# Sparse attention into a Mish MLP on one core: how the first batch's v is read, and where the second batch's steps stand

## Chip, cores and metric

One core of one Trainium2 chip runs the whole kernel. The metric is the device time of one execution in microseconds (us), lower is better; the time given is the median of several executions. All times inside an execution are counted from the start of the profiled span.

## What is computed

Eight batches of eight heads, 576 tokens, head width 64. Heads 0 to 3 are "local": a token sees itself and the 31 tokens before it. Heads 4 to 7 are "strided": a token sees those at or before it with the same position modulo 32. The attention output, 4608 tokens of 512 features, goes through an MLP with 2048 hidden features. Cut to what matters:

```
mask_local   = (rel >= 0) & (rel < 32)
mask_strided = (rel >= 0) & (pos[None, :] % 32 == pos[:, None] % 32)
attn = exp(scores - max) / (sum + 1e-9)          # scores masked, scale 1/8
x = (attn @ v) as [4608, 512]
h = x @ w_in;  out = (h * tanh(softplus(h))) @ w_out
```

## The kernel before

**Tiling.** The tokens go through the MLP in nine blocks of 512 (loop over `t`, L724). A block is MLP1 (`mlp1`, L543: eight groups `g` of 256 hidden features, each 8 matmuls of 512 columns into one of three PSUM accumulators, then one Mish on ScalarE, L562) and MLP2 (`mlp2`, L571: sixteen groups of four matmuls into two of the accumulators). The four 128-feature slices `cc` of MLP1 are two local ones (0, 1) and two strided ones (2, 3); the order is 2, 3, 0, 1. While the MLP of block `t` runs, the attention of batch `t+1` is put between its matmul groups: a hand-written list of sixteen steps (`attn_steps`, L476) gives, for each MLP2 group, what follows it on the engines. Each engine works through its instructions strictly in the order in which they were written.

**Attention of a batch.** `t_step` (L230) and `t_step_loc0` (L248) transpose q and k on TensorE into a PSUM tile `tr` and have it copied to `kTs`, `qTs`, `kTl`, `qTl`. `qk` (L302) makes the scores and has ScalarE take the exponential into `Ps` (strided) or `Pl` (local). `mask` (L342) multiplies by a 0/1 mask on VectorE; for batch 0 `bias` (L292) adds the mask as a matmul beforehand instead. `pv` and `pv2` (L367, L379) multiply by v. The v tiles have 65 columns a head: 64 of v and one of ones, so that the 65th column of the product `po` is the softmax denominator; VectorE takes its reciprocal (`rden`) and multiplies (`x_s`, `x_l`). `xt` (L393) transposes the result into `xT`, the MLP's input. The PSUM tiles `tr`, `po` of `pv`, `trx` and `fill` share two buffers in turn: a third one waits until the first has been read.

**Local windows.** For the local heads the queries are cut into six windows of 96, and the v tile `vl` holds 128 rows a window: rows 32 to 127 are the window's own (one DMA a head brings them for all windows), rows 0 to 31 are the last 32 of the window before, copied over from rows 96 to 127 (`rows_v_loc01`, L141).

**Batch 0 (L618 to L702)** comes before any MLP work can start. Its loads are issued by GpSimd (POOL) in a fixed order: strided k, q, v, local k, q, local v, then the weights and batch 1. Strided v lands as bf16 in `vsd`, a view of `vs32`; `copy_v_str01` (L145) copies it on VectorE into the 65-column tile `vs`. POOL has eight landing semaphores in turn, so an issue waits until the eighth issue before it has landed. `fill` matmuls (L525) do no work of the result; they stand where TensorE would wait.

**Batch 1** has its q and k transposes on TensorE too (`t_steps1`, L266): the strided four stand in MLP1 of block 0 (L758 to L760), two after group 6 and two after group 7, the last; the local four follow the third and the fourth MLP2 group. From batch 2 on, DMAs transpose (`str_by_dma`, `loc_by_dma`).

Of the kernel before, what the change touches and what calls it, by code (L numbers as in the profile page):

```python
# [12 lines left out]
AF = mybir.ActivationFunctionType  # L13
# [3 lines left out]
NW = 6  # L17
WQ = 96
# [22 lines left out]
def kernel(ctx, tc, q, k, v, moe_w_in, moe_w_out, out):  # L41
# [63 lines left out]
                dst[b % 2][0:PN], src[b, 4:8].rearrange("h (p j) d -> p h (j d)", j=CS)  # L105
            )

    def load_str01(dst, src, b, h0=0):
        for p in (slice(0, 64), slice(64, PN)):
            nc.gpsimd.dma_start(  # L110
                dst[p, h0:4], src[b, 4 + h0:8].rearrange("h (p j) d -> p h (j d)", j=CS)[p]
            )

    def load_qk_loc(b):
# [23 lines left out]
                vl[b % 2][32:128, :, h, 0:D], v[b, h].rearrange("(w p) d -> p w d", p=WQ)  # L138
            )

    def rows_v_loc01(b, hp, eng):  # L141
        x = vl[b % 2][:, :, 2 * hp:2 * hp + 2, 0:D]
        cast(eng, x[0:32, 1:NW], x[96:128, 0:NW - 1])

    def copy_v_str01(b, eng, j0, j1):  # L145
        cast(
# [140 lines left out]
    class Attn:  # L287
# [63 lines left out]

        def pv_mm(self, kind, i, po):
            for h in range(4):
                if kind == "l":
# [7 lines left out]
                nc.tensor.matmul(  # L362
                    po[:, h, :], lhsT=pt[0:n, c0:c0 + 128], rhs=rhs,
                    start=True, stop=True,
                )
# [110 lines left out]
    def attn_steps(b, x, y, z=None):  # L476

        a = Attn(b)
        Q = lambda i_acc, *parts: (lambda: a.qk(parts, i_acc))
        M = lambda kd, i: (lambda: a.mask(kd, i, nc.vector))  # L480
        V = lambda kd, i: (lambda: a.pv(kd, i))
        X = lambda kd, hf: (lambda: a.xt(kd, hf))
        s0, s1, sl2, l0, l1 = ("s", 0), ("s", 1), (("s", 2), ("l", 2)), ("l", 0), ("l", 1)
        if x == y:
            return [
                [], [Q(x, s0)],
                [M(*s0), Q(x, s1)],
                [V("s", 0)],
                [V("s", 1), M(*s1), Q(x, *sl2)],
                [V("s", 2)],  # L490
                [V("s", 3), M("s", 2), M("l", 2), Q(x, l0)],
                [V("s", 4)],
                [V("s", 5), M(*l0), Q(x, l1)],
                [V("s", 6), V("l", 5)],
                [V("s", 7), V("l", 0), M(*l1)],
                [X("s", 0), V("l", 1)],
                [X("s", 1), V("l", 2)],
                [V("l", 3), V("l", 4)],
                [X("l", 0), X("l", 1)], [],
            ]  # L500
# [21 lines left out]
        return r  # L522


    def fill(t, n):  # L525
# [17 lines left out]
    def mlp1(t, accs):  # L543
        gT = g_pool.tile([128, 16, 512], BF16, tag="gT", name="gT")

        held = {}

        def group(g, ccs=(2, 3, 0, 1), us=(0, 1)):
            if g not in held:
                held[g] = acc(accs[g % 3], "psh")  # L550
            ps = held[g]
            for u in us:
                fc = 2 * g + u
                for a, n, o in segs(t):
                    for cc in ccs:
                        nc.tensor.matmul(  # L556
                            ps[:, u, o:o + n], lhsT=w_in[:, cc, fc * 128:(fc + 1) * 128],
                            rhs=xT[:, cc, a:a + n], start=(cc == 2 and o == 0),
                            stop=(cc == 1 and o + n == 512),
                        )  # L560
            if ccs[-1] == 1 and us[-1] == 1:
                nc.scalar.activation(gT[:, 2 * g:2 * g + 2, :], ps[:], AF.Mish)  # L562
        if t == 0:
            return gT, [lambda g=g, c=c: group(g, c) for c in ((2, 3), (0, 1)) for g in range(2)] + [
                lambda g=g: group(g) for g in range(2, 8)
            ]
# [49 lines left out]
    with tc.manual_schedule():  # L616
# [26 lines left out]
        Dv.memset(kTs[0][:, 0:16 * SU].rearrange("p (u n) -> p u n", n=SU)[:, :, PN:], 0.0)  # L643
        Dv.memset(kTs[0][:, 16 * SU:], 0.0)
# [59 lines left out]
        for x in (ks, qs):  # L704
            Dv.memset(x[0][64:SU], 0.0)
        load_qk_str(2)
        for hp in range(2):
            rows_v_loc01(1, hp, Po)
        for dst, src in ((kl, k), (ql, q)):
            to = by_tile(dst[0])  # L710
            for h in range(4):
# [4 lines left out]
        load_v_loc_h(2)  # L716

        def next_loads():
            load_qk_str(3)
            copy_v_str01(2, Po, 0, CS)  # L720
            for hp in range(2):
                rows_v_loc01(2, hp, Po)

        for t in range(NBLK):  # L724
            x, y, z = accs
            if t > 0:
                gT, g1 = mlp1(t, accs)
            ts, at, a1 = [], [], []
            if t == 0:
                ts, at = t_steps1(), attn_steps(1, y, y)  # L730
                at[0] += [lambda: Sc.preload_act_table(AF.Exp)]
                at[0] += [lambda x=x: Dv.memset(x[1][64:SU], 0.0) for x in (ks, qs)]
                at[1] += [lambda: copy_v_str01(1, nc.vector, 0, CS), next_loads]
                at[2] += ts[4:6]
                at[3] += ts[6:8]
                at[9] += [lambda: str_by_dma(2), lambda: loc_by_dma(2)]
                out_accs, accs = (z, x), (y, z, x)
            else:
                if t <= 2:
                    at = attn_steps(t + 1, x, y, z if t == 2 else None)  # L740
                elif t + 1 < B:
                    a1 = str_steps(t + 1)
                    at = loc_steps(t + 1, x, y)
                if t == 1:
                    at[9].append(lambda: str_by_dma(3))
                if t == 2:
                    Dv.memset(x_s[64:96], 0.0)
                if t + 2 < B:
                    at[9].append(lambda: loc_by_dma(t + 2))
                if 1 < t < B - 3:  # L750
                    at[9].append(lambda: str_by_dma(t + 3))
                out_accs, accs = (z, y), (z, x, y)
            for i, g in enumerate(g1):
                g()
                if i < len(a1):
                    for s in a1[i]:
                        s()
                if t == 0:  # L758
                    for n in {6: (0, 1), 7: (2, 3)}.get(i, ()):
                        ts[n]()  # L760
            if t > 0 and t + 2 < B:
                cast_qk_loc(t + 2, Po, Po)
                if 1 < t < B - 3:
# [50 lines left out]
```

## Time and profile before

| | |
|---|---|
| median of 7 runs | 306.63 us (305.76 to 309.08) |
| the profiled execution's own time | 306.01 us |
| its span, first to last instruction | 304.2 us (1.8 us lie around it) |
| TensorE busy | 296.7 us, 98% of the span |
| VectorE / ScalarE / GpSimd busy | 160.5 / 180.6 / 99.9 us |
| one MLP matmul of 512 columns, start to start | 0.2158 us (64 of them in 13.81 us) |

PE is TensorE, DVE is VectorE, ACT is ScalarE, POOL is GpSimd. In a timeline row stand: start, length, engine, line, operation, what it writes and reads, shapes, how many were merged, and in brackets the idle time of the engine before it with what ended it. A matmul's length includes its way through the array; where many follow each other, the distance of their starts is what they cost.

### The profile page before, as it was taken

The page shows a single profiled execution, that of the slowest core. Times are in us where ns is not written, and L with a number is a line of the kernel's source. Part 1 is how long each engine was busy: PE and PEld are TensorE (multiplying, and loading weights), DVE is VectorE, ACT ScalarE, POOL GpSimd, SP SyncE. Part 2 cuts the span into 40 slices and gives each one's busy share as a digit, 9 for nine tenths or more (in the row PEclk, how much of TensorE's full clock was granted, in tenths as well). Part 3 has the DMA queues.
Part 4 walks back from the last instruction along what each step waited for, and adds up shares of the span by engine and source line. Part 5 has one row for each costly group of instructions (what it writes and reads, how often), then busy time and mean ns, then how long its engine had stood idle before and what let it go on. Part 6 is the DMA issues. An engine that isn't in the chain of part 4 may idle for free.

```text
span 304.2 us, 5877 instructions
## 1 busy us (share of the span) xinstructions
PE 296.7 (98%) x2430; PEld 154.5 (51%) x2430; DVE 160.5 (53%) x380; ACT 180.6 (59%) x192; POOL 99.9 (33%) x117
## 2 busy tenths in 40 slices
PE   8979999999999999999999999999999999999995
PEld 3544555544454455445488554445444444444444
DVE  4681478102840087588878887798878850000000
ACT  2676643766466755756965796578668756116501
POOL 8742429530245035403960394028600000000000
PEclk9999999999999999999999999999999999999999
DMA  8999999999898999999969998797520120011011
GB/s 140 161 206 188 203 182 134 142 116 222 170 210 134 224 158 200 216 188 186 163 151 199 188 158 148 148 194 130 133 84 0 64 76 0 2 69 69 0 71 69
DMA packets 97006, 41.81 MB, mean 137 GB/s; under 512 B 79572, under 2 KB 90916, under 8 KB 96980
## 3 DMA queue, kind: packets, MB, share of 16 engines
q1 hardware_dynamic: 71708, 28.84, 53.1%
q0 software_dynamic: 24960, 12.31, 34.7%
q8 instruction: 19, 0.31, 0.5%
q10 hardware_dynamic: 312, 0.28, 0.3%
q14 instruction: 7, 0.06, 0.1%
HBM read 36.82 MB, written 9.44 MB: 152 GB/s over the span
## 4 chain that ended last, share of the span: by engine, by line
PE 89%; DVE 3%; DMA 2%; POOL 2%; issue 1%; ACT 1%; DVEq 0%; ACTq 0%; POOLq 0%
PE psh L556 41%; PE pso L579 35%; PE pso L606 5%; PE po L362 4%; PE ps L324 3%; DMA vl<-in_v_dram 2%; DVE x_l L374 1%; DVE x_s L374 1%; PE trx L401 1%; POOL vl L137 1%; DVE rden L373 1%; POOL ks L110 0%; DVE Pl L346 0%; ACT Ps L338 0%; POOL qs L110 0%
## 5 line engine op out<-in xcount | busy, mean ns | idle before, releaser
L556 PE MATMUL psh<-xT,w_in 128*128 128x512 bf16 (+1 forms) x640 | 130.6, 358 | 1.0 <-ACT xT L179 0.7
L579 PE MATMUL pso<-w_out,gT 128*128 128x512 bf16 x512 | 121.7, 379 | 0.0
L562 ACT ACTIVATE gT<-psh 128x1024 bf16<-128x1024 f32 x72 | 72.5, 1024 | 47.2 <-PE psh L556 47.2
L556 PEld LDWEIGHTS <-w_in 128*128 128x128 bf16 x640 | 60.2, 98 | 56.5 <-issue 1.4
L579 PEld LDWEIGHTS <-gT 128*128 128x128 bf16 x512 | 45.5, 98 | 45.9
L436 DVE STREAM_TRANSPOSE xs_t<-x_s 32x512 bf16<-32x512 bf16 x48 | 33.7, 702 | 0.9
L586 ACT COPY osb<-pso 128x1024 f32<-128x1024 f32 x16 | 17.6, 1097 | 24.7 <-PE pso L579 14.1
L373 DVE RECIPROCAL rden<-po 72x4 f32<-72x4 f32 (+1 forms) x98 | 17.2, 176 | 26.4 <-PE po L362 26.1
L181 POOL CAST kl<-kl 96x768 bf16<-96x768 f32 x10 | 8.8, 905 | 64.5 <-DMA kl<-in_k_dram 56.1
L181 DVE COPY osb<-pso 128x512 f32<-128x512 f32 (+1 forms) x2 | 1.1, 558 | 51.3 <-PE pso L606 51.3
L346 DVE TENSOR_TENSOR Ps<-Ps,consts_sb 72x864 bf16<-72x864 bf16 (+3 forms) x12 | 8.0, 675 | 37.7 <-ACT Ps L338 37.7
L427 DVE STREAM_TRANSPOSE xT<-x_l 32x384 bf16<-32x384 bf16 x48 | 27.3, 569 | 0.7
L374 DVE TENSOR_TENSOR x_s<-po,rden 72x256 bf16<-72x256 f32 x56 | 23.5, 420 | 1.9
L338 ACT ACTIVATE Ps<-ps 72x864 bf16<-72x864 f32 (+3 forms) x21 | 17.4, 861 | 10.4 <-PE ps L324 10.3
L443 ACT COPY xT<-xs_t 128x576 bf16<-128x576 bf16 x8 | 21.4, 2938 | 0.0
L362 PEld LDWEIGHTS <-Ps 72*128 72x128 bf16 x256 | 14.8, 98 | 11.6 <-DVE Ps L346 0.8
L338 ACT ACTIVATE Pl<-ps 128x960 bf16<-128x960 f32 (+1 forms) x20 | 17.1, 876 | 4.0 <-PE ps L324 3.9
L374 DVE TENSOR_TENSOR x_l<-po,rden 96x256 bf16<-96x256 f32 x42 | 17.6, 420 | 1.4
L179 ACT COPY xT<-trx 128x576 bf16<-128x576 bf16 x15 | 9.5, 641 | 14.1 <-PE trx L411 11.4
L362 PE MATMUL po<-vs,Ps 72*128 72x65 bf16 x256 | 17.3, 194 | 0.1
L181 POOL CAST vl<-vl 128x768 bf16<-128x768 f32 (+2 forms) x20 | 15.4, 771 | 4.1 <-DMA vl<-in_v_dram 3.1
L346 POOL TENSOR_TENSOR Ps<-Ps,consts_sb 72x1008 bf16<-72x1008 bf16 (+1 forms) x9 | 14.5, 1645 | 0.1
(91 smaller groups left out, 233.4 us busy)
## 6 DMA issues: line engine op xcount, KB each, us to landing
out_dram<-osb SPq DMA_DIRECT2D x16, 512.0 KB, 4.4
kl<-in_k_dram SPq DMA_DIRECT2D x5, 576.0 KB, 6.9
ql<-in_q_dram SPq DMA_DIRECT2D x5, 576.0 KB, 11.5
vs<-in_v_dram SPq DMA_DIRECT2D x5, 576.0 KB
vl<-in_v_dram SPq DMA_DIRECT2D x5, 576.0 KB, 9.6
w_in<-in_moe_w_in_dram POOLq DMA_DIRECT2D x4, 512.0 KB, 11.1
w_out<-in_moe_w_out_dram POOLq DMA_DIRECT2D x4, 512.0 KB, 15.6
ks<-in_k_dram POOLq DMA_DIRECT2D x7, 288.0 KB, 9.4
```

Of the source, the lines that this page charges most:

```text
L181: eng.tensor_copy(out_, in_)
L338: nc.scalar.activation(pt[0:n, :, 0:nw], t[0:n, :, o0:o0 + nw], AF.Exp, scale=scale)
L346: meng.tensor_tensor(out=pm, in0=pm, in1=mk[0:n, :].unsqueeze(1).unsqueeze(1).to_broadcast([n, 2, nu, w]), op=ALU.mult,)
L362: nc.tensor.matmul(po[:, h, :], lhsT=pt[0:n, c0:c0 + 128], rhs=rhs, start=True, stop=True,)
L373: nc.vector.reciprocal(rden[0:m, :], po[0:m, :, D])
L374: nc.vector.tensor_tensor(out=dst.rearrange("p (h d) -> p h d", h=4), in0=po[0:m, :, 0:D], in1=rden[0:m, :].unsqueeze(2).to_broadcast([m, ...
L427: nc.vector.transpose(dst[32 * q:32 * q + 32, :, :, m:m + 32], src[m:m + 32, :, :, q, :])
L436: nc.vector.transpose(xs_t[32 * q:32 * q + 32, :, :, m:m + 32], src[m:m + 32, :, :, q, :])
L443: nc.scalar.copy(xT[:, 2 + c, t0:t0 + S].rearrange("p (n j) -> p j n", j=CS), xs_t[:, :, c, 0:PN])
L556: nc.tensor.matmul(ps[:, u, o:o + n], lhsT=w_in[:, cc, fc * 128:(fc + 1) * 128], rhs=xT[:, cc, a:a + n], start=(cc == 2 and o == 0), stop= ...
L562: nc.scalar.activation(gT[:, 2 * g:2 * g + 2, :], ps[:], AF.Mish)
L579: nc.tensor.matmul(p[:, ot % 2, :], lhsT=gT[:, fc, 128 * ot:128 * ot + 128], rhs=w_out[:, fc, :], start=(fc == 0), stop=(fc == 15),)
```

## The change

Five things are altered, all of them for batches 0 and 1:

1. **Strided v of batch 0** is read by the matmul as it landed (`vsd`, 64 columns); a second matmul of one column, against a column of ones in `vl`, makes the denominator. The two VectorE copies into `vs` go.
2. **Local v of batch 0** is loaded a window at a time (six DMAs of 96 x 4 x 64 in place of four of 96 x 6 x 64); the row copy is made in two parts, windows 0 to 2 before `xt("s")`, windows 3 to 5 after the first local `pv2`. For batches 1 and 2 one copy on POOL replaces two.
3. **MLP1 of block 0**: for groups 0 and 1 the local slices are done in two token pieces, of 288 and of 224 columns.
4. **Loads**: the second half of batch 0's strided k is one DMA of 72 rows in place of 64 and 8; the first quarter of `w_in` is two DMAs; the first part of `w_out` moves ahead of batch 1's k and q, the second ahead of its local k and q.
5. **Batch 1's list** is its own (`attn_steps1`): the four strided transposes follow the first MLP2 group, the four local ones stand after groups 6 to 8, local scores come singly at groups 9 to 11. The two memsets of `ks[1]`, `qs[1]` go from VectorE to POOL. Batch 0's first `kTl` copy goes from VectorE to ScalarE, and its local bias and score matmuls alternate.

```diff
+    def load_v_loc01(b, w0, w1):
+        for w in range(w0, w1):
+            nc.gpsimd.dma_start(
+                vl[b][32:128, w, :, 0:D], v[b, 0:4, WQ * w:WQ * w + WQ].rearrange("h p d -> p h d")
+            )
-    def rows_v_loc01(b, hp, eng):
-        x = vl[b % 2][:, :, 2 * hp:2 * hp + 2, 0:D]
-        cast(eng, x[0:32, 1:NW], x[96:128, 0:NW - 1])
+    def rows_v_loc01(b, w0, w1, eng):
+        w0, x = max(w0, 1), vl[b % 2]
+        cast(eng, x[0:32, w0:w1, :, 0:D], x[96:128, w0 - 1:w1 - 1, :, 0:D])
...
+                    if self.b == 0:
+                        v0 = D * (CS * h + i)
+                        rhs, tail = vsd[0][:, v0:v0 + D], vl[0][0:PN, 1, 0, D:D + 1]
...
+                if tail is not None:
+                    nc.tensor.matmul(
+                        po[:, h, D:D + 1], lhsT=pt[0:n, c0:c0 + 128], rhs=tail,
+                        start=True, stop=True,
+                    )
...
+        return [
+            [lambda: nc.scalar.preload_act_table(AF.Exp)] + ts[0:4],
+            [Q(y, ("s", 0)), lambda: copy_v_str01(1, nc.vector, 0, CS)],
+            [M("s", 0), Q(y, ("s", 1))],
+            [V("s", 0)],
+            [V("s", 1), M("s", 1), Q(y, ("s", 2))],
+            [V("s", 2), ts[4]],
+            [V("s", 3), M("s", 2), ts[6], ts[5]],
+            [V("s", 4), ts[7]],
+            [V("s", 5), Q(y, ("l", 0))],
+            [V("s", 6), M("l", 0), Q(y, ("l", 1))],
+            [V("s", 7), V("l", 0), M("l", 1), Q(y, ("l", 2))],
+            [X("s", 0), V("l", 1), M("l", 2)],
+            [X("s", 1), V("l", 2)],
+            [V("l", 3), V("l", 5)],
+            [V("l", 4), X("l", 0)],
+            [X("l", 1)],
+        ]
...
+            parts = (0, 288, 0), (288, 224, 288)
+            return gT, [lambda g=g: group(g, (2, 3)) for g in range(2)] + [
+                lambda g=g, p=p: group(g, (0, 1), part=p) for p in parts for g in range(2)
+            ] + [lambda g=g: group(g) for g in range(2, 8)]
...
-        load_str01(ks[0], k, 0, 2)
+        nc.gpsimd.dma_start(ks[0][0:PN, 2:4], k[0, 6:8].rearrange("h (p j) d -> p h (j d)", j=CS))
...
-        load_v_loc_h(0)
-        for f in range(0, 2048, 512):
-            load_w_in(f, f + 512)
+        load_v_loc01(0, 0, NW)
+        for f0, f1 in ((0, 256), (256, 512), (512, 1024), (1024, 1536), (1536, 2048)):
+            load_w_in(f0, f1)
+        load_w_out(0, 1)
         load_qk_str(1)
-        load_w_out(0, 1)
         load_v_str01(1)
+        load_w_out(1, 2)
         load_qk_loc01(1, rows(kl[1]), rows(ql[1]))
-        load_w_out(1, 3)
+        load_w_out(2, 3)
...
-        copy_v_str01(0, Dv, 0, 4)
-        copy_v_str01(0, Dv, 4, 8)
...
-        t_step_loc0(kl0, kTl[:, 0, 32:32 + S], 0, Dv)
+        t_step_loc0(kl0, kTl[:, 0, 32:32 + S], 0, Sc)
...
-        a.bias("l", 0, 1)
-        a.bias("l", 1, 2)
-        a.qk([("l", 0)], 1)
-        a.qk([("l", 1)], 2)
-        a.bias("l", 2, 0)
-        a.qk([("l", 2)], 0)
-        for hp in range(2):
-            rows_v_loc01(0, hp, Dv)
+        for i in range(3):
+            a.bias("l", i, (1, 2, 0)[i])
+            a.qk([("l", i)], (1, 2, 0)[i])
+        rows_v_loc01(0, 0, 3, Dv)
...
         a.pv2("l", 0, 1)
+        rows_v_loc01(0, 3, NW, Dv)
         a.pv2("l", 2, 0)
...
         def next_loads():
+            for x in (ks, qs):
+                Po.memset(x[1][64:SU], 0.0)
...
-                at[0] += [lambda x=x: Dv.memset(x[1][64:SU], 0.0) for x in (ks, qs)]
-                at[9] += [lambda: str_by_dma(2), lambda: loc_by_dma(2)]
+                at[10] += [lambda: str_by_dma(2), lambda: loc_by_dma(2)]
```

More of the change, by code (lines that the diff above doesn't have):

```diff
@@ L106, in load_qk_str, with load_str01 @@
             )
-    def load_str01(dst, src, b, h0=0):
+    def load_str01(dst, src, b):
         for p in (slice(0, 64), slice(64, PN)):
             nc.gpsimd.dma_start(
-                dst[p, h0:4], src[b, 4 + h0:8].rearrange("h (p j) d -> p h (j d)", j=CS)[p]
+                dst[p], src[b, 4:8].rearrange("h (p j) d -> p h (j d)", j=CS)[p]
             )
@@ L353, in pv_mm @@
             for h in range(4):
+                tail = None
                 if kind == "l":
@@ L361, in pv_mm @@
                     pt, c0 = P_s[part][:, i % 2], PN * u
+                    if self.b == 0:
+                        v0 = D * (CS * h + i)
+                        rhs, tail = vsd[0][:, v0:v0 + D], vl[0][0:PN, 1, 0, D:D + 1]
                 nc.tensor.matmul(
-                    po[:, h, :], lhsT=pt[0:n, c0:c0 + 128], rhs=rhs,
+                    po[:, h, 0:rhs.shape[-1]], lhsT=pt[0:n, c0:c0 + 128], rhs=rhs,
                     start=True, stop=True,
                 )
+                if tail is not None:
[3 more added lines that the diff above has]
+                    )
         def pv(self, kind, i):
@@ L483, in attn_steps @@
         s0, s1, sl2, l0, l1 = ("s", 0), ("s", 1), (("s", 2), ("l", 2)), ("l", 0), ("l", 1)
[L484 to L500, printed above, removed]
         r = [
@@ L522, in attn_steps, with attn_steps1 @@
         return r
+    def attn_steps1(y, ts):
+        a = Attn(1)
+        Q = lambda i_acc, *parts: (lambda: a.qk(parts, i_acc))
+        M = lambda kd, i: (lambda: a.mask(kd, i, nc.vector))
+        V = lambda kd, i: (lambda: a.pv(kd, i))
+        X = lambda kd, hf: (lambda: a.xt(kd, hf))
+        return [
[16 more added lines that the diff above has]
+        ]
     def fill(t, n):
@@ L546, in mlp1, with group @@
         held = {}
-        def group(g, ccs=(2, 3, 0, 1), us=(0, 1)):
+        def group(g, ccs=(2, 3, 0, 1), us=(0, 1), part=None):
             if g not in held:
@@ L553, in group @@
                 fc = 2 * g + u
-                for a, n, o in segs(t):
+                for a, n, o in segs(t) if part is None else [part]:
                     for cc in ccs:
@@ L560, in group @@
                         )
-            if ccs[-1] == 1 and us[-1] == 1:
+            if ccs[-1] == 1 and us[-1] == 1 and (part is None or part[2]):
                 nc.scalar.activation(gT[:, 2 * g:2 * g + 2, :], ps[:], AF.Mish)
         if t == 0:
-            return gT, [lambda g=g, c=c: group(g, c) for c in ((2, 3), (0, 1)) for g in range(2)] + [
-                lambda g=g: group(g) for g in range(2, 8)
-            ]
+            parts = (0, 288, 0), (288, 224, 288)
+            return gT, [lambda g=g: group(g, (2, 3)) for g in range(2)] + [
+                lambda g=g, p=p: group(g, (0, 1), part=p) for p in parts for g in range(2)
+            ] + [lambda g=g: group(g) for g in range(2, 8)]
         return gT, [lambda g=g, c=c: group(g, c) for c in ((2, 3), (0, 1)) for g in range(3)] + [
@@ L706 @@
         load_qk_str(2)
-        for hp in range(2):
-            rows_v_loc01(1, hp, Po)
+        rows_v_loc01(1, 0, NW, Po)
         for dst, src in ((kl, k), (ql, q)):
@@ L718, in next_loads @@
         def next_loads():
+            for x in (ks, qs):
+                Po.memset(x[1][64:SU], 0.0)
             load_qk_str(3)
             copy_v_str01(2, Po, 0, CS)
-            for hp in range(2):
-                rows_v_loc01(2, hp, Po)
+            rows_v_loc01(2, 0, NW, Po)
         for t in range(NBLK):
@@ L727 @@
                 gT, g1 = mlp1(t, accs)
-            ts, at, a1 = [], [], []
+            at, a1 = [], []
             if t == 0:
-                ts, at = t_steps1(), attn_steps(1, y, y)
-                at[0] += [lambda: Sc.preload_act_table(AF.Exp)]
-                at[0] += [lambda x=x: Dv.memset(x[1][64:SU], 0.0) for x in (ks, qs)]
-                at[1] += [lambda: copy_v_str01(1, nc.vector, 0, CS), next_loads]
-                at[2] += ts[4:6]
-                at[3] += ts[6:8]
-                at[9] += [lambda: str_by_dma(2), lambda: loc_by_dma(2)]
+                at = attn_steps1(y, t_steps1())
+                at[1].append(next_loads)
+                at[10] += [lambda: str_by_dma(2), lambda: loc_by_dma(2)]
                 out_accs, accs = (z, x), (y, z, x)
@@ L757 @@
                         s()
-                if t == 0:
-                    for n in {6: (0, 1), 7: (2, 3)}.get(i, ()):
-                        ts[n]()
             if t > 0 and t + 2 < B:
```

## The prediction

> **What bounds the kernel now.** I read the slices of the page first, then the page's chain, then the stretches, the waits of TensorE, and last the timeline.
>
> ```profile
> PE   8979999999999999999999999999999999999995
> PEclk9999999999999999999999999999999999999999
> PE 89%; DVE 3%; DMA 2%; POOL 2%; issue 1%; ACT 1%; DVEq 0%; ACTq 0%; POOLq 0%
> ```
>
> TensorE is busy in every slice, at full clock, and is 89% of the chain that ended last. Only TensorE's idle time, or work added to it, can move the end.
>
> ```profile
> 0.00:10.60 10.60, 9.21 (x87) 4.36 (x87) 4.60 (x22) 3.46 (x5) 9.55 (x18) 1.00 0.92 147
> 10.60:21.50 10.90, 9.00 (x171) 6.10 (x172) 9.64 (x19) 8.39 (x12) 6.20 (x9) 1.00 1.48 186
> 21.50:34.70 13.20, 13.15 (x89) 6.54 (x89) 2.66 (x5) 7.40 (x8) 3.75 (x6) 1.00 1.31 193
> 34.70:56.10 21.40, 20.81 (x257) 11.68 (x254) 16.06 (x41) 11.24 (x15) 13.74 (x19) 1.00 1.59 167
> ```
>
> Columns: stretch, length, then busy time of PE, PEld, DVE, ACT, POOL. The change lies in rows two to four (batch 0's attention, MLP1 of block 0, MLP2 of block 0 with batch 1). PE idles 1.9 us in the second, 0.6 in the fourth. Matmul ends are modelled, so I also went by starts: between 34.7 and 56.1 starts come late for a reason other than the matmul before them by 1.36 us, five times (0.24, 0.12, 0.51, 0.31, 0.18), and 0.1 us is lost at each switch to or from the narrow score and q/k transposes.
>
> ```profile
> PE psh L556 <- ACT xT L179: 0.7, 1, 0.7
> PE po L362 <- ACT Pl L338: 0.7, 1, 0.7
> PE tr L253 <- DVE x_s L374: 0.3, 1, 0.3
> ```
>
> The first is the stall before MLP1's local slices that the token pieces aim at; the last is a PSUM buffer not yet read. The copies of strided v, which the change removes, hold nobody: they end at 9.91, and the first `po` at 10.64 waits for ScalarE's exponential.
>
> **Stage A, up to the first whole MLP1 group** (before: 21.55 plus eight matmuls of 0.2158, 23.28).
>
> ```profile
> 10.64 0.42 PE L362 MATMUL po<-vs,Ps 72*128 72x65 bf16 x8
> 13.11 1.18 ACT L179 COPY qTl<-tr 128x576 bf16<-128x576 bf16 x2 [0.60 <-PE tr L253]
> 14.41 0.56 PE L297 MATMUL ps<-consts_sb 128*128 128x480 bf16 x2 [0.27 <-DVE x_s L388]
> 15.22 1.38 DVE L181 COPY vl<-vl 32x640 bf16<-32x640 bf16 x2
> 20.86 0.64 ACT L179 COPY xT<-trx 128x576 bf16<-128x576 bf16 x1 [0.48 <-PE trx L401]
> ```
>
> *Ones column.* 32 more matmuls, each with its own weight load in the instruction order. No row has one column. Above: the `po` row, (0.42 - 0.19)/7 = 0.033 us each, 1.06 in all. Below: nothing, if they pass in the shadow of weight loads. I take 0.033, because a `po` matmul of 65 columns is the nearest row. So each `pv2` is 0.26 longer. The waits for the q/k loads (0.23 and 0.15) swallow part; the fourth strided `pv2` starts at 13.8 instead of 13.25.
> *`kTl` copy to ScalarE.* It fills ScalarE's 0.60 idle before `qTl`: both `kTl` copies 11.87 to 13.07, `qTl` until 14.8 (before 14.29). First local scores at 14.87 (before 14.90), so the exponentials start at 15.3 as before.
> *Bias alternating.* The second pair of 480 columns (0.42 with its switch) stood in that wait; now it follows the first scores. The transposes of `x_s` go from 15.90 to 16.40, VectorE's `xT` from 16.53 to 16.88, the first `x_l` ends at 18.43 instead of 18.09 (+0.34).
> *Row copy in two parts.* The row gives 0.595 and 0.650 for 640 elements, so about 0.5 for windows 0 to 2 (512 elements), hidden while VectorE waits for `xT`; and 0.72 for windows 3 to 5 (768). The latter now stands between the first and second `rden`, and TensorE's second local `pv2` (window 3) waits for it: 18.35 to 19.07, then 0.39 until the next `rden`. Second `x_l` 20.38 (before 18.98), third 21.22 (before 19.81).
> *TensorE behind it.* First two strided MLP1 groups at 19.53 and 20.70 (before 18.42, 19.54), the transposes of `x_l` after each, the last at 21.56 (before 20.40). Token pieces: the first piece's `xT` is ready at 21.55, so the 0.71 stall is gone and MLP1 goes on at 21.82; 8 x (288 columns, 0.1225) + 8 x (224, 0.096) = 1.75 against 1.73. Whole groups from 23.57: **+0.30**. With the ones columns free the same steps give 22.98, -0.30.
> *Loads.* One DMA of 72 rows for k: the 64 and 8 row pieces landed at 5.11 and 5.82, and are wanted at 6.27 behind the `fill`s; nothing lost. [...] Local v landed last at 15.86 before; its wait (0.14 on VectorE) goes, nothing else hangs on it.
>
> **Stage B, MLP1 to the end of MLP2 of block 0** (before 23.28 to 56.13). MLP1's 48 whole matmuls cost 10.36 in both; the four strided transposes (4 x 0.26) change place.
>
> ```profile
> 31.91 0.42 PE L237 MATMUL tr<-consts_sb,ks 72*128 72x72 bf16 x8
> 32.37 0.46 DVE L181 COPY kTs<-tr 128x576 bf16<-128x576 bf16 x1 [8.72 <-PE tr L237]
> 40.85 0.45 PE L253 MATMUL tr<-consts_sb,ql 96*64 96x96 bf16 x12 [0.35 <-DVE x_s L374]
> 45.33 0.72 POOL L181 COPY vl<-vl 32x640 bf16<-32x640 bf16 x1 [0.89 <-DMA vl<-in_v_dram]
> 45.45 0.91 DVE L346 TENSOR_TENSOR Ps<-Ps,consts_sb 72x576 bf16<-72x576 bf16 x1
> ```
>
> *Four transposes in a row.* They have two PSUM buffers. Start s: the first's copy begins s + 0.46 and ends s + 0.92 (rows one and two), and TensorE follows a read buffer by 0.06 (14.35 to 14.41 in stage A): the third starts at s + 0.98, but TensorE was ready at s + 0.52, 0.46 lost. The second copy ends 0.37 after the first, so the fourth waits 0.11 more. Before, MLP1 groups stood between the pairs. **+0.57**, a new wait, with all of MLP2 behind it.
> *The list.* Going through it with the rows' lengths (pso group 0.863; `po` 0.13; `rden` 0.18, `x_s` 0.42; `kTl` 0.74; masks 0.59, 0.64; TensorE to VectorE 0.23), from the fourth transpose on: 0.09 before the second strided scores, 0.14 before the third `pv` (mask), 0.53 before the first `ql` transposes (buffer not read), 0.06 before the second local scores, 0.30 before the first `trx` of `x_l` (buffer). Sum with 0.57: 1.7, against 1.36 before: +0.35. Nine excursions to narrow matmuls instead of six and a half: 5 more switches of 0.1, +0.5. The 1.98 us of memsets leave VectorE, but the second MLP2 group and the exponential end later than VectorE there, so they bring nothing; on POOL they stand before loads whose transposes start at 88.05, over 9 us after landing (78.69). **+0.8**; between +0.3 (only the transposes, switches hidden) and +1.2.
> *Order of loads.* `w_out`'s first part (landed 33.63, wanted at 34.7) goes ahead of batch 1's k and q (29.23, 31.51; wanted at 31.9). The same bytes then land by about 33.6, wanted from 34.8 on; the two `w_in` quarters have smaller packets, bounded by the 768-byte loads of 1.5 to 2.1 us for 288 KB. No wait.
> *Later batches.* The DMA transposes of batch 2 follow one group later, with TensorE equally late: nothing.
>
> Sum: 0.30 + 0.8 = **+1.1 us** on 306.01, 307.1. The profiled run lay 0.6 under the median of 306.63; against that I predict **307.7**.
>
> **Rivals.** *POOL's single row copy meets a mask (slower).* The last row above: while POOL copied (45.33 to 46.05) the 576-element mask took 0.91, though 864 elements take 0.59; it looks held until POOL ended. The change has one copy of 1280 elements (1.44). By my times the mask runs at 44.7, the copy from 45.3, after local v's last landing (45.21). If TensorE is 0.6 later or v earlier, the mask ends at 47.1, the second `kTl` copy behind it at 47.9, and the `pv` that needs its buffer waits from 46.06: +1.9, in all +3.0, 309.6. For: the gap is small. Against: the same bytes precede local v. [...]
> *Loads late (slower).* If batch 1's q lands at 35.5 instead of 33.6, the transposes start 0.5 late: +1.6, 308.2.
> *Ones columns free, switches hidden.* Stage A -0.3, stage B +0.3: 306.6, no change.
> *The stalls really go (faster).* If stage A's idle 1.9 falls to 0.5 and stage B stays: -1.4, 305.2. Against: the row copy and the two-buffer wait, which the order on VectorE and TensorE shows.
>
> **Chances.** Forecast 0.52 (306.9 to 308.4); free columns 0.18; faster rival 0.10, two thirds of it beyond -0.5%; POOL 0.12; loads 0.08. Half a percent is 1.5 us, about what a measurement can tell from no change: faster 0.07, same 0.63, slower 0.30 (POOL, half of the loads, and the top of the forecast). Range 305.5 to 309.4: it leaves out most of the faster rival and the top of POOL's.
>
> **What would show it.** Whole MLP1 groups start near 23.6; no wait of `psh` for `xT`; VectorE's second row copy between two local `rden` and TensorE's `po` waiting for it; about half a microsecond of TensorE waiting for `kTs` copies near 35.5; MLP1 of block 1 from about 57.2 instead of 56.13. Wrong if ones columns start under 0.02 apart, or if the second row copy ends before 18.6.

## The result, and the profile after

The changed kernel takes **307.98 us** in the median (25 runs, 306.73 to 311.68); the kernel before, on the same chips, 306.64 (62 runs, 305.68 to 310.91). The ratio is **1.0050, with a 95% interval of 1.0035 to 1.0065**: about 1.5 us longer. The forecast was 307.7.

The profiled execution of the changed kernel took 309.12 us and so lay above its median; a second profile of the same code, called e1 below, took 307.69. Both are shown, and the working goes by e1. Of some kernels a part of the runs had a lower granted TensorE clock (0.987 to 0.994 in the mean, the others 0.998 or more; in the profiles of f1 to f4 0.50 for 3.41 us or twice that); that is the subject of the run g1, and medians are of all runs unless the text says otherwise.

First the page of the changed kernel, the slices and the chain:

```profile
PE   8889999999999998999999999999999999999995
PE 90%; DVE 4%; DMA 2%; issue 1%; POOL 1%; ACT 1%; ACTq 0%; POOLq 0%
```

TensorE still sets the end. Then the last three of the four stretches shown of before, cut at the same events (first `po`, in MLP1, first `pso`, block 1's MLP1; length, busy time of PE, PEld, DVE, ACT, POOL, granted clock, DMA share, GB/s). The changed kernel's first profile:

```profile
10.90:21.50 10.60, 8.36 (x187) 5.96 (x188) 6.54 (x16) 7.80 (x11) 8.58 (x12) 1.00 1.38 155
21.50:35.00 13.50, 13.50 (x81) 7.15 (x80) 3.98 (x6) 8.34 (x9) 3.57 (x5) 1.00 1.24 194
35.00:58.57 23.57, 22.59 (x285) 13.23 (x284) 14.53 (x41) 11.42 (x15) 16.05 (x20) 1.00 1.54 179
```

and e1:

```profile
10.95:21.50 10.55, 9.25 (x198) 6.51 (x198) 7.44 (x18) 8.21 (x12) 8.16 (x12) 1.00 1.50 172
21.50:33.86 12.36, 12.36 (x71) 6.51 (x70) 3.14 (x3) 7.70 (x8) 3.15 (x5) 1.00 1.31 193
33.86:57.44 23.58, 22.59 (x286) 13.24 (x285) 14.53 (x41) 11.43 (x15) 13.98 (x19) 1.00 1.60 170
```

The last stretch is the same in both, 23.57 and 23.58; it now holds all four strided transposes. The two profiles differ in the two rows above it. The waits of TensorE from 10 to 58 us say why; the first lines of each list, e1 first, then the first profile:

```profile
PE po L372 <- DVE vl L187: 1.1, 1, 1.1
PE tr L259 <- DVE x_s L389: 0.4, 1, 0.4
PE tr L243 <- DVE kTs L187: 0.3, 1, 0.3
```

```profile
PE po L372 <- DVE vl L187: 1.2, 1, 1.2
PE tr L259 <- DMA lq<-in_k_dram: 0.7, 1, 0.7
```

The wait of `psh` for `xT` is gone. Two new ones stand there: `po` for VectorE's row copy (`vl`, L187), and `tr` for the copies `kTs`. The wait for the load `lq` is in the first profile and not in e1 (local k landed at 12.20 there, at 10.94 in e1), and e4 below, with the loads of before, has one of 0.5: it belongs to that execution.

By the starts of the matmuls, stage A (to the first whole MLP1 group) and stage B (from there to block 1's MLP1):

| | first `po` | whole groups | block 1's MLP1 | stage B |
|---|---|---|---|---|
| before | 10.64 | 23.27 | 56.13 | 32.86 |
| after, first profile | 10.94 | 24.64 | 58.57 | 33.93 |
| after, e1 | 10.99 | 23.50 | 57.44 | 33.94 |
| forecast | 10.64 | 23.57 | 57.2 | 33.6 |

### The profile page after: what moved, and what is told of

Its sections match the earlier page's. It is cut to its first block, busy times and chain, and to the rows that moved or that the text cites. A ratio compares the mean times of both kernels' runs of the same rounds, so it can differ in the third digit from the quotient of the medians.

```text
span 307.4 us, 5958 instructions
## 1 busy us (share of the span) xinstructions
PE 298.1 (97%) x2470; PEld 156.3 (51%) x2470; DVE 155.5 (51%) x375; ACT 181.6 (59%) x193; POOL 103.0 (34%) x119
## 4 chain that ended last, share of the span: by engine, by line
PE 90%; DVE 4%; DMA 2%; issue 1%; POOL 1%; ACT 1%; ACTq 0%; POOLq 0%
PE psh L581 40%; PE pso L605 34%; PE po L372 5%; PE pso L632 5%; PE ps L330 3%; DMA lq<-in_k_dram 2%; DVE x_l L389 1%; PE tr L259 1%; PE trx L416 1%; DVE x_s L389 1%; DVE Pl L352 1%; DVE rden L388 1%; PE trx L426 0%; ACT Ps L344 0%; POOL qs L110 0%
## 5 line engine op out<-in xcount | busy, mean ns | idle before, releaser
L581 PE MATMUL psh<-xT,w_in 128*128 128x512 bf16 (+3 forms) x648 | 130.5, 355 | 0.3 <-ACT Ps L344 0.3
L187 POOL CAST kl<-kl 96x768 bf16<-96x768 f32 x10 | 7.9, 820 | 66.0 <-DMA kl<-in_k_dram 66.0
L187 DVE COPY osb<-pso 128x512 f32<-128x512 f32 (+1 forms) x2 | 1.1, 558 | 51.3 <-PE pso L632 51.3
L352 DVE TENSOR_TENSOR Ps<-Ps,consts_sb 72x864 bf16<-72x864 bf16 (+3 forms) x12 | 6.7, 559 | 39.1 <-ACT Ps L344 39.1
L372 PEld LDWEIGHTS <-Ps 72*128 72x128 bf16 x256 | 15.6, 97 | 11.6 <-DVE Ps L352 0.8
L372 PE MATMUL po<-vs,Ps 72*128 72x65 bf16 (+1 forms) x256 | 18.1, 194 | 0.1
L187 POOL CAST vl<-vl 128x768 bf16<-128x768 f32 (+2 forms) x20 | 15.4, 770 | 3.2 <-PE po L372 2.0
```

Source lines behind the costliest of these rows:

```text
L187: eng.tensor_copy(out_, in_)
L352: meng.tensor_tensor(out=pm, in0=pm, in1=mk[0:n, :].unsqueeze(1).unsqueeze(1).to_broadcast([n, 2, nu, w]), op=ALU.mult,)
L372: nc.tensor.matmul(po[:, h, 0:rhs.shape[-1]], lhsT=pt[0:n, c0:c0 + 128], rhs=rhs, start=True, stop=True,)
L581: nc.tensor.matmul(ps[:, u, o:o + n], lhsT=w_in[:, cc, fc * 128:(fc + 1) * 128], rhs=xT[:, cc, a:a + n], start=(cc == 2 and o == 0), stop= ...
```

## Experiments

The question behind them: is the loss the two new waits and the switches (my theory), or do loads, ones columns and the order of the biases carry it (the rivals)? None of them leaves work out; g1 and g4 have TensorE do matmuls that nobody reads. Each ratio is to the kernel before, run in between on the same chip.

| run | median us | ratio, 95% | runs with clock 0.994 or less |
|---|---|---|---|
| e1, the change once more | 307.69 (1 run) | | 0 of 1 |
| e2, batch 1's list back | 307.01 | 1.0009, 0.9984 to 1.0033 | 3 of 12 |
| e3, second row copy early | 307.00 | 1.0008, 0.9986 to 1.0031 | 0 of 12 |
| e4, token pieces alone | 305.88 | 0.9970, 0.9933 to 1.0008 | 3 of 12 |
| f1, k in 64 and 8 rows | 308.01 | 1.0054, 1.0028 to 1.0080 | 4 of 12 |
| f2, no ones column | 307.49 | 1.0043, 1.0018 to 1.0067 | 3 of 12 |
| f3, biases first | 308.08 | 1.0054, 1.0031 to 1.0078 | 3 of 12 |
| f4, transposes in pairs | 308.68 | 1.0050, 1.0020 to 1.0081 | 6 of 12 |
| g1, fills in the wait | 307.67 | 1.0034, 1.0011 to 1.0056 | 0 of 12 |
| g2, e2 and e3 together | 306.20 | 0.9984, 0.9963 to 1.0006 | 0 of 12 |
| g3, and no ones column | 305.96 | 0.9988, 0.9967 to 1.0010 | 1 of 12 |
| g4, token pieces and fills | 306.64 | 1.0008, 0.9984 to 1.0032 | 4 of 12 |

Of the changed kernel itself 8 of 26 runs had the lower clock, of the kernel before, run beside these, 12 of 99.

**e1_after_again.** No edit.

> The changed kernel once more, for a second profile. Theory (row copy in two parts, transposes in a row, more switches): the same three waits as in the first profile, about 1.0 us or more before the second local po, 0.57 for the kTs buffers, 0.6 before the first ql transposes. Rival (loads): if the 0.85 us wait for the local k load (landed 12.20, before 11.08) is there again, the late loads belong to the change; if it is under 0.3, they belonged to that execution and the profile overstates stage A by about that much.

It shows which parts of the first profile repeat: the row copy's wait and the whole of stage B, not the wait for the load.

**e2_list_back.** Batch 1's list, its memsets and the loads' order as before:

```diff
-                at = attn_steps1(y, t_steps1())
+                ts, at = t_steps1(), attn_steps(1, y, y)
...
+                    for n in {8: (0, 1), 9: (2, 3)}.get(i, ()):
+                        ts[n]()
```

> The changed kernel with batch 1's list of steps, its memsets and the order of the loads of batch 1 and w_out as they were before; all of batch 0 as changed. Theory: stage B costs 0.8 (0.57 for the four transposes in a row, the rest switches), so this gains 0.8 on the changed kernel: 0.5 us over before, ratio 1.0015. Rival (stage A carries the whole loss, stage B nothing): no gain, ratio 1.005.

Stage B is 32.87 again, 1.07 less than in e1, and the median falls by 1.0. List, memsets and load order together cost what stage B shows, and nothing later takes it back; the three were not taken apart.

**e3_row_copy_early.** The second row copy behind the first, before VectorE's `xT`:

```diff
         rows_v_loc01(0, 0, 3, Dv)
+        rows_v_loc01(0, 3, NW, Dv)
...
         a.pv2("l", 0, 1)
-        rows_v_loc01(0, 3, NW, Dv)
```

> The changed kernel with the second row copy (windows 3 to 5) right behind the first, ahead of the transposes of x_s, in VectorE's idle time. Theory: TensorE's wait of 1.33 us for that copy falls to what ScalarE's exponential leaves (0.3 or less), so 0.7 to 1.0 us are gained on the changed kernel: ratio about 1.002. Rival (the local v of windows 3 to 5 lands too late anyway, 17.0 in the profile, or TensorE is held by something else): under 0.3 gained, ratio 1.004 to 1.005.

The median falls by 1.0. VectorE's timeline of e3 around the copies:

```profile
15.67 0.81 DVE L187 COPY vl<-vl 32x512 bf16<-32x512 bf16 x2
17.18 0.76 DVE L187 COPY xT<-trx 128x576 bf16<-128x576 bf16 x1 [0.70 <-PE trx L426]
```

Both copies (the row names the first's shape) fit into the time in which VectorE waits for `trx`, and 0.70 us of it is left over. TensorE's second local `pv2` no longer waits for `vl`; the third waits 0.6 us for `x_l` instead, so the whole groups start 0.41 earlier than in e1, not 1.3. Of the rest some 0.2 is the clock (g1: without the runs at the lower clock the changed kernel's median is 307.8); the remainder these profiles do not account for.

**e4_pieces_only.** The kernel before with MLP1's token pieces and nothing else:

```diff
+            parts = (0, 288, 0), (288, 224, 288)
...
+                lambda g=g, p=p: group(g, (0, 1), part=p) for p in parts for g in range(2)
```

> The kernel before with the token pieces alone (local slices of MLP1's groups 0 and 1 of block 0 in 288 and 224 columns). Theory: the 0.71 us stall for xT goes and nothing comes in its place: 0.6 to 0.7 us faster than before, ratio 0.998. Rival (eight more matmuls and a new wait for the second piece eat it): ratio 1.000.

Whole groups start at 22.58 instead of 23.27, 0.69 earlier; the median is 0.9 under that of before by the ratio, with an interval that just takes in no change. TensorE's timeline, before and then e4:

```profile
20.40 0.42 PE L401 MATMUL trx<-consts_sb,x_l 96*128 96x96 bf16 x6
21.55 1.02 PE L556 MATMUL psh<-xT,w_in 128*128 128x512 bf16 x4 [0.73 <-ACT xT L179]
```

```profile
20.58 0.42 PE L401 MATMUL trx<-consts_sb,x_l 96*128 96x96 bf16 x6
20.84 2.13 PE L556 MATMUL psh<-xT,w_in 128*128 128x288 bf16 x17
```

After the last transposes the local slices follow at once: the first piece needs only the tokens whose `xT` is already there, and ScalarE copies the others meanwhile. By the trace this part of the change is a gain of 0.69 us; the interval of the time alone does not settle it.

**f1_k_64_8.** Strided k's second half in two DMAs again.

```diff
-        nc.gpsimd.dma_start(ks[0][0:PN, 2:4], k[0, 6:8].rearrange("h (p j) d -> p h (j d)", j=CS))
+        for p in (slice(0, 64), slice(64, PN)):
+            nc.gpsimd.dma_start(ks[0][p, 2:4], k[0, 6:8].rearrange(...)[p])
```

> The kernel after, with the second half of batch 0's strided k loaded in two pieces again, 64 and 8 rows, as before the change; all else of the change stays. Theory (the 72-row DMA costs the start of the kernel, though the prediction put it at nothing): in both profiles of the changed kernel the strided q landed at 7.5 and 7.8 us and TensorE's first po came at 10.94 and 10.99, against 7.34 and 10.64 before. So q lands near 7.35 again, the first po comes at 10.65 to 10.75, and everything behind it 0.3 earlier: about -0.3 us on the changed kernel, 0.3 of its +1.5 over the kernel before. Rival (the later start has another reason, the removed copies of v or the loads behind it): first po stays at 10.95, no change of the time.

The rival holds. The median does not move, and the first `po` came at 11.66, later than in any other profile. Over the 14 profiles the first `po` follows the landing of strided q by 3.1 to 3.4 us, and q lands anywhere from 7.08 (g1, with one DMA for k) to 8.52 (f1, with two). My two later starts in the changed kernel were scatter; I had read a cause into them.

**f2_no_ones_column.** Strided v copied into the 65-column tile, as before.

```diff
-                    if self.b == 0:
-                        v0 = D * (CS * h + i)
-                        rhs, tail = vsd[0][:, v0:v0 + D], vl[0][0:PN, 1, 0, D:D + 1]
...
+        copy_v_str01(0, Dv, 0, 4)
+        copy_v_str01(0, Dv, 4, 8)
```

> The kernel after, with the strided v of batch 0 copied by VectorE into the tile with the ones column again (two copies, as before), so that the 32 matmuls of one column fall away; all else of the change stays. Theory (the ones column is work added to TensorE): a strided pv2 of batch 0 takes 0.23 instead of 0.43 us, 4 x 0.20 = 0.8 less of TensorE's work; part of it lies in front of the waits for the local k and q and for ScalarE's exponentials, so MLP1's whole groups start 0.2 to 0.5 earlier. Rival (the columns pass in waits that are there anyway): whole groups start where they do in the changed kernel, within 0.1. Second rival: VectorE's copies hold the first pv2, and the gain is given back there.

Window 3 of the second local `pv2` starts at 18.89 instead of 19.13 (e1), 0.24 earlier of the 0.8 that TensorE is spared; the copies hold nobody. In this execution local k and q landed at 11.40 and 13.05 (e1: 10.94 and 12.56), and their transposes start right behind, at 11.44 and 13.10; so the loads took a part of the gain, and 0.24 is not its upper end. From the local q transposes to the `x_s` transposes it is 3.29 us with and without the columns, so there they lie in a wait. The median is 0.5 lower, but the intervals of the two ratios overlap.

**f3_bias_first.** The biases in the order of before:

```diff
-        for i in range(3):
-            a.bias("l", i, (1, 2, 0)[i])
-            a.qk([("l", i)], (1, 2, 0)[i])
+        a.bias("l", 0, 1)
+        a.bias("l", 1, 2)
+        a.qk([("l", 0)], 1)
...
```

> The kernel after, with the local bias matmuls in the order of before (two biases, two score groups, then the third of each) instead of alternating; all else of the change stays. Theory (the second bias stood in the wait for the copies of qTl, and alternating puts its 0.42 us behind them): the transposes of x_s start 0.4 earlier (16.63 in the changed kernel), VectorE's first x_l follows, whole groups 0.3 to 0.4 earlier, the time -0.3 to -0.4. Rival (ScalarE's exponentials set that end, not TensorE's scores): the transposes may move, but first local pv2 and whole groups stay within 0.1.

The gain does not show. TensorE in f3, from the local q transposes on:

```profile
13.57 0.70 PE L259 MATMUL tr<-consts_sb,lq 96*64 96x96 bf16 x24
14.65 0.97 PE L303 MATMUL ps<-consts_sb 128*128 128x480 bf16 x4
15.55 0.56 PE L330 MATMUL ps<-qTl,kTl 64*128 64x96 bf16 x18
16.83 0.22 PE L330 MATMUL ps<-qTl,kTl 64*128 64x96 bf16 x2 [0.72 <-issue]
```

The first scores come 1.98 us after those transposes; in e1 it is 1.58 (13.34 to 14.92). With the ones columns the fourth strided `pv2` ends so late that only one bias fits in front of `qTl`, so a second one delays the scores, and ScalarE's first exponential by 0.31 (2.41 behind the transposes, 2.10 in e1). The `x_s` transposes follow after 3.88 instead of 3.29, but that is not the order's doing alone: the last row has a gap of 0.72 before the last two scores of the second group, for which the profile names no wait, and the changed kernel's first profile has one of 0.23 in front of the same two matmuls (3.70 there). What the order costs at that place this profile cannot say. The kernel before, with the biases first, needs 3.28 (12.62 to 15.90), as e1 does, and the median of f3 is no lower: no run shows a cost of the alternating order, though the interval of the ratio, 0.0024 to either side, could hide 0.3 us.

**f4_pairs.** The strided transposes of batch 1 two and two:

```diff
-            [lambda: nc.scalar.preload_act_table(AF.Exp)] + ts[0:4],
+            [lambda: nc.scalar.preload_act_table(AF.Exp)] + ts[2:4],
...
+                if t == 0 and i == 9:
+                    ts[0]()
+                    ts[1]()
```

> The kernel after, with the four strided q/k transposes of batch 1 in two pairs: two behind MLP1's sixth whole-or-pieced group pair (two groups before its end), two behind the first MLP2 group, instead of four in a row behind the first MLP2 group; all else of the change stays. Theory (two PSUM buffers for four transposes: a wait of 0.45 and 0.11 us measured in the changed kernel near 35.5): both waits go, -0.55 us, and one more switch to narrow matmuls of 0.1 comes: -0.45 in all, MLP1 of block 1 that much earlier. Rival (the wait is only taken over by the next stall of the list, the local ql transposes waiting for their buffer): within 0.1 of the changed kernel.

By the trace the theory holds to 0.1: stage B is 33.38 (24.97 to 58.35) against 33.94, 0.56 less for a forecast of 0.45, and the wait of `tr` for `kTs` is not in the list any more. Both waits go whole; the extra switch, priced at 0.1, is not seen. The median shows nothing of it, since half of the runs had the lower clock; the six others have one of 307.4, the 18 such runs of the changed kernel 307.8, and the eight of f1, on the same chip, 307.6. So the time agrees in the sign and does not show the size.

**g1_fill_in_wait.** Five idle matmuls in the wait for the row copy:

```diff
         a.pv2("l", 0, 1)
+        fill_acc(2, 5)
         rows_v_loc01(0, 3, NW, Dv)
```

> The kernel after, with five matmuls of 512 columns on data that nobody reads, put on TensorE between the first and the second local pv2, where it waits 1.3 us for VectorE's second row copy; nothing else is changed, so the wait itself stays. Theory (the clock gate): in four profiles of relatives of the changed kernel (f1, f2, f3, f4) the granted clock fell to 0.50 for 3.41 us, or twice that, at 19.1 to 20.9 us, always at the end of a stretch of 3.41 us in which matmuls streamed for under half of the time (38% to 48%); where that share stayed at 51% or more it did not fall. The fills bring 1.08 us of streaming into the wait, so no such stretch is left: the granted clock of the runs stays at 0.998 or more in all or all but one of the runs with a time, where 8 of 26 of the changed kernel lay at 0.994 or less, and these cost about 1.9 us each; the other runs stay at about 307.7. So the median goes from 308.0 to about 307.7 and the upper tail goes. Rival (the falls come from late loads at the start, and not from this wait): 3 or 4 of the 12 runs have the lower clock still, the median stays. Second rival: the fills delay the second pv2, and all times are 0.2 to 1 us longer.

None of the 12 runs had the lower clock, and the median is 307.67, as the theory had it. What it is about, in stretches of f1 and then of g1 (last columns: granted clock, DMA share, GB/s):

```profile
17.51:20.93 3.42, 1.83 (x41) 1.45 (x39) 2.68 (x6) 2.63 (x4) 2.34 (x4) 1.00 1.24 203
20.93:24.34 3.41, 3.41 (x19) 1.73 (x18) 2.86 (x5) 0.64 (x1) 0.71 (x2) 0.50 1.24 205
```

```profile
15.54:18.95 3.41, 3.01 (x58) 2.08 (x52) 1.96 (x5) 3.37 (x5) 3.41 (x5) 1.00 1.20 169
18.95:22.37 3.42, 3.42 (x36) 2.26 (x33) 2.99 (x5) 1.28 (x2) 0.77 (x2) 1.00 1.23 204
```

In f1 the wait for the row copy leaves TensorE busy for 1.83 of 3.42 us; in the 3.41 us after it the granted clock is 0.50, and matmuls of 512 columns start 0.43 apart (22.20, 22.63, 23.05) in place of 0.22. Three more profiles (f2, f3, f4) show the same at 19.1 to 19.5 us, f3 for two such lengths; in f3 only the first 0.5 us of the wait lies in the stretch before the fall, together with the gap of 0.72. The kernels that have the wait unfilled (the changed one, e1, e2, f1 to f4) had the lower clock in 27 of 87 runs; those that fill it or copy early (e3, g1, g2, g3) in 1 of 48. So the new wait costs more than its length. In the changed kernel the 8 runs have a median of 309.8, the other 18 one of 307.8: 2.0 us each.

**g2_list_and_row_copy.** The edits of e2 and e3 together.

> The kernel after with two parts undone together: batch 1's list, memsets and load order as before (as in e2), and the second row copy right behind the first (as in e3). Theory (two places, two costs that add up): e2 measured 1.0 and e3 1.0 less than the changed kernel's 308.0, so together about 306.0, 0.7 under the kernel before; whole MLP1 groups near 23.1, block 1's MLP1 near 56.0. Rival (one hides the other): 306.6 to 307.0.

306.20: the two add up. The ratio fell by 0.0066, 2.0 us, from the changed kernel to this one. Whole groups 23.32, block 1's MLP1 56.57: stage B is 33.25, 0.38 longer than in e2, and here a load holds it. TensorE's first `ql` transposes wait for batch 1's local q (0.2 in the list of waits) and start 0.65 behind the `kl` ones (38.34 to 38.99), in e2 0.28 (38.91 to 39.19). With the same list g3 has 32.88.

**g3_also_no_ones.** g2 with the edit of f2.

> As g2_list_and_row_copy, and the ones column undone too (VectorE copies strided v, no matmuls of one column); of the change stay the copy of kTl on ScalarE, the alternating biases, the row copy by windows, the loads and the token pieces. Theory (the ones column is 0.2 to 0.5 us of stage A, as f2 showed): 305.5 to 305.8, under both kernels; this is the candidate for the best version beside the token pieces alone (305.88). Rival (behind the early row copy another wait swallows the gain, as ScalarE's exponentials do in the token pieces alone): as g2, within 0.15.

305.96, between the forecast and the rival, and the shortest span of any profile, 303.2. It is no better than the token pieces alone (305.88): what else the change holds (`kTl` on ScalarE, the alternating biases, local v by windows) moves nothing that can be measured. Neither e4 nor g3 is faster than the kernel before beyond its interval.

**g4_pieces_and_fill.** e4 with two idle matmuls behind the first local `pv2` (`fill_acc(2, 2)`).

> The kernel before with the token pieces alone (as e4), and two matmuls of 512 columns on data that nobody reads between the first and the second local pv2, where TensorE waits 0.9 us for ScalarE's last local exponential. Theory (the clock gate): e4 had 3 of 12 runs at a lower clock though no stretch of its own profile falls under 57%, so loads that land later must have brought them there; 0.43 us more of streaming puts the share of that stretch up by 12 points, and 0 or 1 of 12 runs have the lower clock; the other runs stay at 305.8. Rival (those falls arise earlier, in the waits for the local k and q): still 2 to 4 of 12.

The rival: 4 of 12 runs still have the lower clock. Nor does any stretch of its own profile explain it. Why e4, g4 and the kernel before meet it in some runs stays open; only the profiled execution of each can be looked into, and none of those three shows it.

## Why the prediction was right, and where it was not

The sum was +1.1 on 306.01, the measured difference +1.1 to +2.0 us (the ratio's interval on 306.64). It is right in direction and nearly so in size. The sum knew nothing of the lower clock: the changed kernel's runs without it have a median of 307.8, for a forecast of 307.7. By steps:

- **Stage A, +0.30 forecast, +0.23 in e1.** The times of the steps agree to some hundredths: whole groups 23.50 for 23.57, first groups at 19.52 and 20.63 for 19.53 and 20.70. That is partly luck. e1's first `po` was 0.35 later by the landing of q, which is scatter; against that two terms were too large. *Ones column:* a `pv2` is 0.20 longer, not 0.26 (below), and only 0.24 in all reached the second local `pv2` in f2; I had 0.6 between the forecast and the case with free columns. *Row copy:* 768 elements took 0.36 us, not 0.72. It began at 18.72 for 18.35, so it ended at 19.08 for 19.07: two errors that cancel. Durations of this copy are no good to scale: 640 elements took 0.60 and 0.65 in the kernel before, 0.36 and 0.49 in e4, and 768 took 0.35 or 0.36 in eight profiles and 0.48, 0.60 and 0.64 in e2, e3 and f1.
- **The place of the row copy** was right, and so was the wait that follows, the largest new one. VectorE and then TensorE in e1:

```profile
18.00 0.69 DVE L403 TENSOR_TENSOR x_l<-po,rden 96x512 bf16<-96x512 f32 x1
18.72 0.36 DVE L187 COPY vl<-vl 32x768 bf16<-32x768 bf16 x1
```

```profile
17.16 0.84 PE L372 MATMUL po<-vl,Pl 128*128 128x65 bf16 x12
19.13 0.55 PE L372 MATMUL po<-vl,Pl 128*128 128x65 bf16 x12 [1.14 <-DVE vl L187]
```

  TensorE waits through `x_l` and the copy. That the clock fell behind this wait as well, to 0.50 in f1, f2 and f4, is missing from the prediction.
- **Token pieces:** the 0.71 us stall goes, as worked out (e4: 0.69).
- **Alternating biases, +0.34:** the cause was wrong. I counted the second bias as moved out of a wait, and did not see that the ones columns of the same change shorten that wait (f3). In e1 the local q transposes start 0.72 later than before (13.34 for 12.62) and the `x_s` transposes 0.73 (16.63 for 15.90): the delay is there ahead of the biases, and between the two none is added. What biases first would give in the changed kernel stays open.
- **Loads:** "nothing lost" for the 72 rows was right (f1). The 72 rows landed at 5.5 to 6.1 us, the 64 rows at 5.0 to 5.3, and the 8 rows at 5.2 to 5.8. So the 72 rows landed 0.7 later in the mean than the 64; the start of the work does not follow it.
- **Stage B, +0.8 forecast, +1.08 in e1.** The four transposes in a row cost 0.45 and 0.11, to the hundredth what I had. TensorE and VectorE in e1:

```profile
34.73 0.42 PE L243 MATMUL tr<-consts_sb,ks 72*128 72x72 bf16 x8
34.99 0.43 PE L243 MATMUL tr<-consts_sb,qs 72*128 72x72 bf16 x8
35.70 0.42 PE L243 MATMUL tr<-consts_sb,ks 72*128 72x72 bf16 x8 [0.29 <-DVE kTs L187]
```

```profile
35.19 0.46 DVE L187 COPY kTs<-tr 128x576 bf16<-128x576 bf16 x1 [10.14 <-PE tr L243]
```

  The third starts 0.05 after the first's buffer is read (35.65). The mis-sized term is *the list*: I summed the late starts to 1.7 us, they are 2.06 (second strided scores 0.24 for 0.09, first `ql` transposes 0.60 for 0.53, second local scores 0.20 for 0.06). So +0.70 instead of +0.35; the switches to narrow matmuls cost about +0.4 for my +0.5. At the strided transposes no switch is lost: the fourth's eight matmuls, 0.033 apart from 36.06, end where the next group starts (36.32).
- **Rivals.** POOL's single row copy met no mask: in e1 it ran from 46.31 to 47.56, after local v's landing, and the last strided mask ended at 45.13. The loads of batch 1 held nobody in the two profiles of the changed kernel (in g2 one did). The ones columns are not free.
- **Made of what:** in medians e4 says about -0.9 for the pieces, e2 and e3 say +1.0 each for the list and for the place of the row copy, f2 +0.2 to +0.5 for the columns: about +1.3 to +1.6, near the +1.5 measured. Each of these has an interval of 0.7 us or more to either side, so the sum is a fit and not a proof.

And the ones columns in e1's timeline:

```profile
10.99 0.20 PE L372 MATMUL po<-vs,Ps 72*128 72x64 bf16 x1
11.03 0.17 PE L377 MATMUL po<-vl,Ps 72*128 72x1 bf16 x1
11.06 0.19 PE L372 MATMUL po<-vs,Ps 72*128 72x64 bf16 x1
```

The two starts of a pair stand about 0.03 apart whether the matmul has 64 columns or one; over 16 matmuls the mean is 0.0287 us. So here, where each has a weight load of its own, a matmul of one column costs as much as one of 64.

## What to carry to other kernels

A change with several parts is costed part by part, and the parts are then looked at for what they do to each other's waits: here one part's gain (the pieces, 0.7 to 0.9 us) was more than paid back by two others that bound a step to a buffer or to an engine's order. A copy goes where its engine waits for something else anyway, not behind work that the same waiting instruction also depends on. One profile's late load is compared with several executions before it gets a cause.

## What the runs showed of the hardware

**The clock fell to 0.50 behind a short wait.** In f1, f2 and f4 the granted clock fell to 0.50 for 3.41 us after a stretch of 3.41 us that held narrow matmuls and the whole wait of TensorE (1.3 to 1.6 us from start to start); in f3, for twice that, after a stretch with a part of the wait and the gap of 0.72. In those four profiles the clock had risen to 1.00 at 7.27, 5.76, 5.46 and 5.87 us, and fell 13.65 us later, four times 3.41; in the kernel before it was 1.00 from 6.27 to 303.23 us, 87 times 3.413. So in these profiles its changes stand whole multiples of 3.41 us apart. In e1 the clock rose at 4.79, so a multiple of 3.41 behind that (18.44) parts the same wait (17.80 to 19.13), and the clock stayed at 1.00. Whether the share of a stretch in which TensorE works decides it isn't settled. In f1, f2, f4 and g2 the record of the first MLP1 matmul behind the wait is missing (three of four stand there, beside four weight loads). With it, and with each matmul counted where it starts (0.2158 us per 512 columns), 45, 46, 47 and 49% of a stretch were followed by a fall (f4, f1, f2, f3) and 52% (e2, g2) was not; with each matmul cut at the edges, 41, 45, 45 and 50% were and 48% (e2, g2) was not.

**Landing of the first loads scatters.** Strided q landed from 7.08 to 8.52 us in 14 profiles, in all of which it is issued right behind strided k. That is as much as the whole change costs.

**Where a mask and a copy met, the later one took longer.** In the first profile of the changed kernel a local mask of a later batch, 960 elements on VectorE, took 1.50 us (117.11 to 118.61) while GpSimd made a copy that had begun before it and took 1.89 us (116.21 to 118.10); the eight masks of this size in e1 took 0.69 in the mean. TensorE then lost 0.87 us, which is part of the 1.4 us between the two profiles' times. In e1 the two met as well, but the mask began 0.03 before the copy (116.52 and 116.55): the mask took 0.64, the copy 2.37 in place of the 1.89 of the four other such copies in e1, and TensorE lost nothing there. In the prediction's rival, too, the copy began first. Whether the hold lasts to the copy's end is not shown: from there the mask took 0.51 in the first profile and 0.31 in the kernel before (46.05 to 46.36), less than such a mask takes in e1 (0.69 in the mean, and 0.44 for 576 elements).
